# First attention chain: Grams of q in a PSUM bank of their own, and S copied by VectorE ahead of the first Exp

## The chip, the cores and the metric

The kernel runs on one core of one Trainium2 chip. The metric is device time in microseconds (us), the median of several runs. Engines are named as in the profile: PE is TensorE's matmul, PEld its weight load, DVE is VectorE, ACT is ScalarE, POOL is GpSimd, SP is SyncE.

## The reference

Four batches b of q, k, v, each 6336 x 256 in float32. Per batch a cross-covariance attention over the 256 channels, and then a highway layer over all 25344 rows:

```
qn = q / (norm(q, axis=1) + 1e-6);  kn = k / (norm(k, axis=1) + 1e-6)
a  = softmax(kn.T @ qn / tau)                     # 256 x 256 for each batch
x  = v @ a
out = T*H + (1-T)*x,  H = relu(x @ w_h),  T = sigmoid(x @ w_t + b_t)
```

## The kernel before, in words

**Tiles.** A batch is 49 slices of 128 rows and a remainder of 64 rows. Loads of q, k and v come in groups of slices (lists QG and VG); GpSimd issues them, and they turn float32 into float16 on the way. Groups of q and of k each go through a ring of 4 tiles, groups of v through a ring of 3. A load into a used tile waits until TensorE has read the tile's earlier contents.

**Scores.** For each slice, `emit_score` (L219) adds two matmuls of 256 columns to S = k.T q (L230), and four of 128 columns to the Gram matrices, two for k (L234) and two for q (L239). Only the diagonals of the Grams are used: they are the squared norms. S fills one PSUM bank, and all four Gram blocks share another bank, G. The last TAIL[0] = 6 slices of batch 0 are taken part by part: first all their q Grams (12 matmuls), then their k Grams (12), then their S (12), so that work on the norms can start before S is complete. For the later batches a part of the squares is summed by ScalarE, GpSimd and VectorE instead (L449, L455, L462).

**The chain of a batch** (`make_chain`, L493) turns S and G into the weights `mr`:

- `nq` and `norms`: VectorE reads the two diagonals of q, and of k (L503).
- `root`: for batch 0 ScalarE takes the square roots (L527), for the other batches GpSimd does.
- `ssb`: ScalarE copies S from PSUM to SBUF (L520).
- `invs`: VectorE adds 1e-6 and takes the reciprocals (L540, L543).
- `table`: ScalarE loads the table of Exp (L491), with a small activation to force it.
- `cq`: TensorE spreads 1/norm of q over the partitions (L549). `logits`: VectorE multiplies S by it (L558).
- `exps`: Exp on ScalarE (L575). `softmax`: VectorE divides by the row sums (L586, L589).
- `at`, `atc`, `ah`, `ahc`: transposes of the weights, and their product with w_h and w_t (L600, L611, L619, L630). Then `back` loads the table of Sigmoid.

**Slots.** After a batch's chain its rows come out in 25 slots of two slices: transposes of v (L293) and their copy to SBUF (L307), then twelve matmuls into the tiles zbank, h and x (L317), Sigmoid on ScalarE (tt, L358), refilling zbank with the bias (L361), two products on VectorE (o, L366; ux, L376), a subtraction on GpSimd (L399), and stores of 1 MB from SP (L416).

**PSUM.** Eight banks: z0, z1, vT (transposes), S and G (batch 0), hx1 and hx2 (S and G of the later batches), and hx0. The tiles cq, at, ah, h and x take whichever of the free banks was freed earliest; the list `banks` (L333) starts with hx0, and S and G of batch 0 join it once `ssb` and `norms` have read them (L1130).

**Order.** Nothing is ordered by hand alone: a planner at the end of the function runs through time in steps of 0.01 us, with a length for each task (for instance 0.62 for `ssb` on ScalarE, L650) and a model of the DMA queue, and emits each engine's instructions in the order in which it would start them. Tasks of a chain stand in a queue per engine and leave it strictly in order; `add` appends them. So ScalarE's chain queue of batch 0 is: root of q, ssb, root of k, table, exps, ... On the chip each engine then executes its own list in that order, and waits where the data is later than the planner thought.

Of the kernel before, what the change touches and what calls it, by code (L numbers as in the profile page):

```python
# [11 lines left out]
f32 = mybir.dt.float32  # L12
# [3 lines left out]
P = 128  # L16
# [44 lines left out]
def kernel(  # L61
# [11 lines left out]
    nc = tc.nc  # L73

    B, N, C = q.shape
# [11 lines left out]
    def spans(*sizes):  # L87
# [37 lines left out]
    psum_pool = ctx.enter_context(  # L125
        tc.tile_pool(name="psum", bufs=1, space=bass.MemoryType.PSUM)
    )
# [4 lines left out]
    def pair_of(t):  # L132
        b, i = divmod(t, NPAIR)
        return b, PAIRS[b][i]

    pairsets, unit_of = [], {}
    for t in range(NSLOT):
        b, i = pair_of(t)
# [17 lines left out]
    PE_LAG, LAG, TO_PE = 0.20, 0.08, 0.10  # L156
# [34 lines left out]
    def tile_of(kind, b, s):  # L191
        if s == NS:
            return tiles["rem", kind][:, b, :]
        groups = (VG if kind == "v" else QG)[b]
        g = group_of(groups, s)
        return tiles[kind, b, g][:, s - groups[g][0], :]
# [13 lines left out]

    S_t, G_t = {}, {}

    squares = {
        (kind, b, j + m) for b in RUNS for kind in "qk" for j in RUNS[b][kind] for m in range(CH)
# [2 lines left out]
    def emit_score(b, j, parts, first, last):  # L219
        if first:  # L220
            tags = ("S", "G") if b == 0 else ("hx1", "hx2")
            S_t[b] = psum_pool.tile([P, 2, C], f32, tag=tags[0], name=f"S{b}")
            G_t[b] = psum_pool.tile([P, 4, P], f32, tag=tags[1], name=f"G{b}")
        nr = REM if j == NS else P
        kk, qq = tile_of("k", b, j), tile_of("q", b, j)
        S, G = S_t[b], G_t[b]
        for c in range(2):
            kc = kk[0:nr, bass.ts(c, P)]
            if "s" in parts:
                nc.tensor.matmul(  # L230
                    S[:, c, :], kc, qq[0:nr, :], start=first and c == 0, stop=last and c == 1
                )
            if "k" in parts:
                nc.tensor.matmul(  # L234
                    G[:, c, :], kc, kc, start=begins(b), stop=False, skip_group_check=True,
                )
        for c in range(2 if "q" in parts else 0):
            qc = qq[0:nr, bass.ts(c, P)]
            nc.tensor.matmul(  # L239
                G[:, 2 + c, :], qc, qc, start=begins(b), stop=False, skip_group_check=True  # L240
            )

    begun = set()

    def begins(b):
        if b in begun:
            return False
        begun.add(b)
        return True

    score, grams, score_tasks, last_score = {}, {}, [], {}
# [78 lines left out]
        def free(self, now):  # L330
            return all(t.end is not None and t.end + LAG <= now for t in self.until)

    banks = [Bank("hx0")]  # L333
    handed = []

    def free_bank(now):
# [153 lines left out]
    def preload_table(func):  # L490
        nc.scalar.activation(out=dummy, in_=ones32[:, 0:1], func=func)  # L491

    def make_chain(b):  # L493
        st = {}
        T = {}
        def norms(kind):
            def emit(e):
                if "n2" not in st:
                    st["n2"] = work_pool.tile([P, 4], f32, tag="n2", name=f"n2_{b}")
                o = 2 if kind == "q" else 0  # L500
                for i in (o, o + 1):
                    junk = work_pool.tile([P, P], f32, tag="junk", bufs=1, name=f"junk{b}_{i}")
                    nc.vector.scalar_tensor_tensor(  # L503
                        out=junk, in0=G_t[b][:, i, :], scalar=0.0, in1=ident0,
                        op0=AluOp.bypass, op1=AluOp.mult, accum_out=st["n2"][:, i : i + 1],
                    )
            return emit
# [9 lines left out]

        def ssb(e):
            st["ssb"] = work_pool.tile([P, 2, C], f32, tag="ssb", bufs=1, name=f"ssb{b}")
            nc.scalar.copy(out=st["ssb"], in_=S_t.pop(b))  # L520

        def root(kind):
            def emit(e):
                o = 2 if kind == "q" else 0
                dst, src = nrm[:, o : o + 2, 0], st["n2"][:, o : o + 2]
                if b == 0:
                    nc.scalar.activation(out=dst, in_=src, func=Act.Sqrt)  # L527
                else:
                    nc.gpsimd.tensor_tensor(
                        out=dst, in0=src, in1=half[:, 0:2], op=AluOp.pow  # L530
                    )
            return emit

        def invs(kind):
            def emit(e):
                o = 2 if kind == "q" else 0
                if "inv" not in st:
                    st["inv"] = work_pool.tile([P, 4], f32, tag="inv", name=f"inv{b}")
                inv = st["inv"][:, o : o + 2]
                nc.vector.tensor_reduce(  # L540
                    out=inv, in_=nrm[:, o : o + 2, :], axis=mybir.AxisListType.X, op=AluOp.add
                )
                nc.vector.reciprocal(out=inv, in_=inv)  # L543
            return emit
# [88 lines left out]
        def add(key, engine, length, emit, after, bank=None):  # L633
            T[key] = Task(("chain", b, key), engine, length, emit, after)
            T[key].wants_bank = bank is not None
            T[key].readers = bank
            queues[engine + ".chain"].append(T[key])
            return T[key]
# [7 lines left out]
        engine, length = ("ACT", 0.25) if b == 0 else ("POOL", 0.75)  # L646
        for kind, n in (("q", "nq"), ("k", "norms")):
            add(("root", kind), engine, length, root(kind), [(T[n], LAG)])
            if kind == "q":
                add("ssb", "ACT", 0.62, ssb, [(last_score[b], PE_LAG)])  # L650
        add(("invs", "q"), "DVE", 0.4, invs("q"), [(T["root", "q"], LAG)])
        add(("invs", "k"), "DVE", 0.4, invs("k"), [(T["root", "k"], LAG)])
        add("table", "ACT", 1.5, lambda e: preload_table(Act.Exp),
            [(T["root", "k"], 0.0)] if b == 0 else [(T["invs", "q"], EXP_LAG)])
        add("cq", "PE", 4 * MM(C), pe_cq, [(T["invs", "q"], TO_PE)],
            bank=lambda: [T["softmax", 0], T["logits", 1]])
# [12 lines left out]
        for c in range(2):  # L669
            add(("at", c), "PE", 2 * MM(P), pe_at(c), [(T["softmax", c], TO_PE)],  # L670
                bank=lambda c=c: [T["atc", c]])
        for c in range(2):
            add(("atc", c), "DVE" if c == 0 else "ACT", 0.4, at_copy(c), [(T["at", c], PE_LAG)])
            add(("ah", c), "PE", 2 * MM(2 * C), pe_ahat(c), [(T["atc", c], TO_PE)],
                bank=lambda c=c: [T["ahc", c]])
# [44 lines left out]
    for t in range(NSLOT):  # L720
        i = pair_of(t)[1]
# [39 lines left out]
    for b in range(B):  # L761
        i = 0
# [35 lines left out]
    ident0 = const_pool.tile([P, P], f32, tag="ident0")  # L798
# [8 lines left out]
    btb = const_pool.tile([P, 2, C], f32, tag="btb")  # L807

    def seed_banks():
        btp = psum_pool.tile([P, 2, C], f32, tag="hx0", name="btp")  # L810
        nc.tensor.matmul(btp[:, 0, :], ones32[0:1, :], bt_sb, start=True, stop=True)
        for u in range(2):
            nc.scalar.copy(out=btb[:, u, :], in_=btp[:, 0, :])
        for i in range(2):
            zb = psum_pool.tile([P, 2, C], f32, tag=f"z{i}", name=f"zbank{i}")
            nc.tensor.matmul(
                zb[:, :, :], zeros[:, 0:P], zeros[:, :], start=True, stop=True,
                skip_group_check=True,
            )
            nc.scalar.copy(out=zb[:, :, :], in_=btb[:, :, :])  # L820
            zbank.append(zb)
# [24 lines left out]
    for b in range(B):  # L846
        queues["PE.S"] += make_scores(b)
        chains[b] = make_chain(b)
# [4 lines left out]
    for t in range(NSLOT):  # L853
        b, i = pair_of(t)
# [94 lines left out]
    def head(n):  # L949
        return queues[n][ptr[n]] if ptr[n] < len(queues[n]) else None  # L950
# [172 lines left out]
    while True:  # L1123
        if not dma.advance(now, STEP):
            idle_dma += STEP
        if not setup_done[0] and score[0, 3].end is not None and score[0, 3].end < now:
            seed_banks()
            preload_table(Act.Sqrt)
            setup_done[0] = True
        for b, key, tag in ((0, "ssb", "S"), (0, "norms", "G"), (B - 1, "ssb", "hx1"),  # L1130
                            (B - 1, "norms", "hx2")):
            if tag not in handed and chains[b][key].end is not None:
                handed.append(tag)
                banks.append(Bank(tag))
                banks[-1].until = [chains[b][key]]
        for e, f in (("PE", step_pe), ("ACT", step_act), ("DVE", step_dve),
                     ("POOL", step_pool), ("SP", step_sp)):
            while free[e] <= now and f(now):
                pass
        finished = all(ptr[n] == len(queues[n]) for n in queues) and nload[0] == len(loads) and \  # L1140
            all(s.dma.end is not None for s in store_tasks)
        if finished:
            break
        now += STEP
        assert now < 600, [(n, head(n).name) for n in queues if head(n) is not None]
# [38 lines left out]
```

## Time and profile before

| what | us |
|---|---|
| median of 3 runs (lowest to highest) | 270.42 (270.23 to 270.47) |
| time of the profiled execution | 270.2 |
| its span, first to last instruction | 268.4 |
| outside the span | 1.8 |
| TensorE clock granted, mean | 0.997 |
| PE / DVE / POOL / ACT busy | 246.2 / 207.8 / 205.3 / 192.5 |

The page of a profile gives the busy time of each engine, a row of 40 slices of the span for each (a digit is the busy share in tenths), and groups of instructions by line. Other views used here are the timeline of one engine (start, duration, line and operation, and in brackets the idle time just before it with the instruction that ended it), the waits (who waited for whom), the chain of work that ended last, in order of time, and a table of engine busy time and DMA rate by stretches of time. Matmuls overlap in the pipe, so the duration of a single one (0.27 us for 256 columns) is longer than the step from one to the next (0.11 us).

In time, batch 0's scores take the first 38 us, paced by loads; its chain runs from about 35 to 45.5 us; the first slot's matmuls begin at 45.72 us; from then on slots of one batch and scores of the next are interleaved, and the last chain (batch 3) ends at about 212 us. The last matmuls end near 263 us.

### The profile page before, as it was taken

To read this page: it belongs to the slowest core of one execution; us is meant where nothing else is said; L and a number is where in the kernel's file an instruction comes from. 1 tells how busy PE (TensorE), PEld (TensorE's weight loads), DVE (VectorE), ACT (ScalarE), POOL (GpSimd) and SP (SyncE) were. 2 spreads that over 40 slices of the span, in tenths; PEclk is the share of its full clock that TensorE was granted. 3 is DMA by queue.
4 is the path that set the end of the run, shared out by engine and by line. 5 is a ranking of instruction groups with operands and counts; after the bars stand their busy time and mean duration, and the time that the engine had idled before them with its cause. 6 is when DMAs were issued, how large, how long until landed. Compare 5 with 4: busy or idle time off the path is not lost.

```text
span 268.4 us, 6454 instructions
## 1 busy us (share of the span) xinstructions
PE 246.2 (92%) x2564; PEld 213.9 (80%) x2564; DVE 207.8 (77%) x415; ACT 192.5 (72%) x320; POOL 205.3 (76%) x182
## 2 busy tenths in 40 slices
PE   0996887899999999979999999999999999999991
PEld 0696785789989997869988987898989687989780
DVE  2000035869999999879989899899999998989895
ACT  3310026969689979869996798898867987888690
POOL 6133455489999999997899998899966485977870
PEclk9999999999999999999999999999999999999998
DMA  7999999999999999999999999999999999698436
GB/s 215 214 214 213 204 187 221 209 214 213 215 210 213 234 268 215 209 271 211 291 289 301 284 215 224 213 297 300 274 290 353 298 375 413 141 224 347 205 128 236
DMA packets 16287, 66.08 MB, mean 246 GB/s; under 512 B 1793, under 2 KB 4610, under 8 KB 13314
## 3 DMA queue, kind: packets, MB, share of 16 engines
q0 software_dynamic: 11040, 38.67, 73.2%
q1 hardware_dynamic: 4930, 26.35, 24.6%
q10 hardware_dynamic: 288, 0.66, 0.7%
q8 instruction: 20, 0.33, 0.4%
q14 instruction: 9, 0.07, 0.1%
HBM read 78.38 MB, written 25.95 MB: 389 GB/s over the span
## 4 chain that ended last, share of the span: by engine, by line
PE 39%; DMA 34%; POOL 10%; DVE 8%; issue 5%; ACT 3%; DVEq 0%; POOLq 0%; ACTq 0%
DMA k<-in_k_dram 19%; DMA v<-in_v_dram 10%; PE x L317 7%; PE zbank L317 7%; PE S L230 7%; PE h L317 7%; POOL o L399 5%; PE vtps L293 4%; DMA out_dram<-o 3%; PE G L234 3%; PE G L239 2%; DVE o L366 2%; DVE ux L376 2%; DMA qk<-in_k_dram 2%; ACT tt L358 1%
## 5 line engine op out<-in xcount | busy, mean ns | idle before, releaser
L399 POOL TENSOR_TENSOR o<-o,ux 128x1024 f32<-128x1024 f32 (+1 forms) x49 | 110.5, 2257 | 24.0 <-DVE ux L376 20.9
L317 PEld LDWEIGHTS <-vts 128*128 128x128 f16 x1200 | 111.7, 98 | 16.4 <-issue 4.3
L230 PE MATMUL S<-q,k 128*128 128x256 f16 x392 | 73.5, 278 | 13.0 <-DMA k<-in_k_dram 6.7
L358 ACT ACTIVATE tt<-zbank 128x512 f32<-128x512 f32 x100 | 59.3, 595 | 23.8 <-PE zbank L317 16.0
L366 DVE SCALAR_TENSOR_TENSOR o<-h,tt 128x512 f32<-128x512 f32 x96 | 65.8, 685 | 6.5 <-ACT tt L358 3.2
L376 DVE SCALAR_TENSOR_TENSOR ux<-tt,x 128x512 f32<-128x512 f32 (+1 forms) x104 | 68.1, 658 | 2.7 <-PE x L317 2.7
L317 PE MATMUL x<-mr,vts 128*128 128x256 f16 (+1 forms) x400 | 60.5, 273 | 0.4 <-DVE o L366 0.4
L317 PE MATMUL zbank<-mr,vts 128*128 128x256 f16 (+1 forms) x400 | 60.5, 273 | 0.0
L317 PE MATMUL h<-mr,vts 128*128 128x256 f16 (+1 forms) x400 | 60.5, 273 | 0.0
L361 ACT COPY zbank<-btb 128x512 f32<-128x512 f32 x98 | 57.6, 591 | 2.7
L230 PEld LDWEIGHTS <-k 128*128 128x128 f16 x392 | 37.6, 100 | 19.0 <-DMA k<-in_k_dram 7.9
L234 PE MATMUL G<-k 128*128 128x128 f16 x256 | 44.0, 224 | 0.7 <-DVE junk L503 0.7
L293 PE MATMUL vtps<-ident,v 128*128 128x128 f16 x392 | 38.3, 219 | 1.0 <-DVE vts L307 0.7
L307 DVE COPY vts<-vtps 128x512 f16<-128x512 f16 x68 | 28.6, 421 | 6.7 <-PE vtps L293 6.3
L293 PEld LDWEIGHTS <-v 128*128 128x128 f16 x392 | 28.7, 98 | 4.5 <-issue 1.7
L177 POOL DMA_DIRECT2D q<-in_q_dram x25 | 14.2, 568 | 23.1 <-PE G L239 18.6
L503 DVE SCALAR_TENSOR_TENSOR junk<-G,ident 128x128 f32<-128x128 f32 x16 | 4.7, 291 | 31.0 <-PE G L234 30.3
L239 PE MATMUL G<-q 128*128 128x128 f16 x216 | 28.6, 224 | 0.0
L455 POOL TENSOR_TENSOR sqq<-sqq 128x512 f32<-128x512 f32 (+1 forms) x22 | 26.4, 1204 | 0.1
L234 PEld LDWEIGHTS <-k 128*128 128x128 f16 x256 | 24.0, 101 | 1.8 <-issue 1.1
L449 ACT ACTIVATE sqq<-q 128x1024 f32<-128x1024 f16 x22 | 23.0, 1054 | 0.0
L462 DVE TENSOR_REDUCE sqq<-sqq 128x256 f32<-128x768 f32 x22 | 22.6, 1027 | 0.0
(78 smaller groups left out, 214.9 us busy)
## 6 DMA issues: line engine op xcount, KB each, us to landing
out_dram<-o SPq DMA_DIRECT2D x23, 1024.0 KB, 9.8
v<-in_v_dram POOLq DMA_DIRECT2D x11, 768.0 KB, 17.2
q<-in_q_dram POOLq DMA_DIRECT2D x7, 768.0 KB, 14.9
k<-in_k_dram POOLq DMA_DIRECT2D x7, 768.0 KB, 19.3
q<-in_q_dram POOLq DMA_DIRECT2D x9, 512.0 KB, 13.3
k<-in_k_dram POOLq DMA_DIRECT2D x9, 512.0 KB, 15.2
v<-in_v_dram POOLq DMA_DIRECT2D x4, 832.0 KB, 19.0
q<-in_q_dram POOLq DMA_DIRECT2D x4, 256.0 KB, 13.0
```

Source lines behind the costliest of these rows:

```text
L230: nc.tensor.matmul(S[:, c, :], kc, qq[0:nr, :], start=first and c == 0, stop=last and c == 1)
L234: nc.tensor.matmul(G[:, c, :], kc, kc, start=begins(b), stop=False, skip_group_check=True,)
L239: nc.tensor.matmul(G[:, 2 + c, :], qc, qc, start=begins(b), stop=False, skip_group_check=True)
L293: nc.tensor.transpose(ps[:, u, c, 0:r], vt[0:r, bass.ts(c, P)], ident[0:r, 0:r])
L307: cp(out=sb, in_=ps)
L317: nc.tensor.matmul(dst[0:r, u, :], vT_t[t][:, u, kt, 0:r], mr[:, kt, off : off + C], start=(not seeded and kt == 0 and (u == 0 or i == NPA ...
L358: nc.scalar.activation(out=tts[t], in_=zbank[t % 2], func=Act.Sigmoid)
L361: nc.scalar.copy(out=zbank[t % 2], in_=btb)
L366: nc.vector.scalar_tensor_tensor(out=ot[pr, o0 + us.start : o0 + us.stop, :], in0=hx["h", t][pr, us, :], scalar=0.0, in1=tts[t][pr, us, :] ...
L376: nc.vector.scalar_tensor_tensor(out=uxs[n][pr, 2 * half + us.start : 2 * half + us.stop, :], in0=tts[t][pr, us, :], scalar=1.0, in1=hx["x ...
L399: ins = sub.tensor_tensor(out=dst, in0=dst, in1=uxs[n][pr, us, :], op=AluOp.subtract)
L455: nc.gpsimd.tensor_tensor(out=sq[:, 1 : 1 + half, :], in0=sq[:, 1 : 1 + half, :], in1=sq[:, 1 + CH - half : 1 + CH, :], op=AluOp.add,)
```

## The change

For batch 0 alone:

- The Grams of q get a tile Gq of their own in the bank hx0; those of k stay in G. Each of the two banks has its own first matmul with `start`. For later batches Gq is the second half of G, as before.
- hx0 is no longer free from the start: it joins the list of banks once `nq` has read Gq.
- `ssb` is done by VectorE, and stands in VectorE's chain queue behind the two `invs`; ScalarE's chain queue is then root of q, root of k, table, exps, ...
- The tile btp, which holds the bias while the seeds are made near 11 us, moves from hx0 to the bank of the transposes, vT.

```diff
@@ emit_score
             G_t[b] = psum_pool.tile([P, 4, P], f32, tag=tags[1], name=f"G{b}")
+            Gq_t[b] = G_t[b][:, 2:4, :] if b else psum_pool.tile(
+                [P, 2, P], f32, tag="hx0", name=f"Gq{b}"
+            )
...
-                    G[:, c, :], kc, kc, start=begins(b), stop=False, skip_group_check=True,
+                    G[:, c, :], kc, kc, start=begins(b, "k"), stop=False, skip_group_check=True,
...
-                G[:, 2 + c, :], qc, qc, start=begins(b), stop=False, skip_group_check=True
+                Gq[:, c, :], qc, qc, start=begins(b, "q"), stop=False, skip_group_check=True
...
-    def begins(b):
-        if b in begun:
+    def begins(b, kind):
+        bank = (b, kind if b == 0 else "")
+        if bank in begun:
             return False
-        begun.add(b)
+        begun.add(bank)
         return True
@@ banks
-    banks = [Bank("hx0")]
+    banks = []
@@ norms
-                        out=junk, in0=G_t[b][:, i, :], scalar=0.0, in1=ident0,
+                        out=junk, in0=Gq_t[b][:, i - 2, :] if i > 1 else G_t[b][:, i, :], scalar=0.0, in1=ident0,
@@ ssb
-            nc.scalar.copy(out=st["ssb"], in_=S_t.pop(b))
+            cp = nc.vector.tensor_copy if e == "DVE" else nc.scalar.copy
+            cp(out=st["ssb"], in_=S_t.pop(b))
@@ make_chain
-            if kind == "q":
+            if kind == "q" and b > 0:
                 add("ssb", "ACT", 0.62, ssb, [(last_score[b], PE_LAG)])
         add(("invs", "q"), "DVE", 0.4, invs("q"), [(T["root", "q"], LAG)])
         add(("invs", "k"), "DVE", 0.4, invs("k"), [(T["root", "k"], LAG)])
+        if b == 0:
+            add("ssb", "DVE", 0.7, ssb, [(last_score[b], PE_LAG)])
@@ seed_banks
-        btp = psum_pool.tile([P, 2, C], f32, tag="hx0", name="btp")
+        btp = psum_pool.tile([P, 2, C], f32, tag="vT", name="btp")
@@ planner's loop
-        for b, key, tag in ((0, "ssb", "S"), (0, "norms", "G"), (B - 1, "ssb", "hx1"),
+        for b, key, tag in ((0, "nq", "hx0"), (0, "ssb", "S"), (0, "norms", "G"), (B - 1, "ssb", "hx1"),
                             (B - 1, "norms", "hx2")):
```

## The prediction

> **What bounds the kernel now.** I read the page's first two parts, then the chain of work that ended last, then the timelines of the engines around batch 0's chain, the waits, and the DMA rate by stretches.
>
> ```profile
> span 268.4 us, 6454 instructions
> PE 246.2 (92%) x2564; PEld 213.9 (80%) x2564; DVE 207.8 (77%) x415; ACT 192.5 (72%) x320; POOL 205.3 (76%) x182
> ...
> PE   0996887899999999979999999999999999999991
> ...
> DMA  7999999999999999999999999999999999698436
> ```
>
> The DMA engines are full from the start to slice 34 (about 228 us), and PE is full from about 57 to 260 us. PE's few idle stretches lie ahead of 58 us, and one at 117 us. So what happens in batch 0's chain matters in two ways: PE's idle time there is part of the total, and any gap in the DMA queue is never made up.
>
> The chain of work that ended last goes straight through the place of the change:
>
> ```profile
> 35.83 0.31 DVE junk L503 x2
> 36.14 0.02 issue
> 36.16 0.31 DVE junk L503 x2
> 36.47 0.04 issue
> 36.51 0.61 PE G L234 x8
> 37.12 0.23 PE S L230 x2
> 37.35 0.29 issue
> 37.64 0.55 POOL q L177
> ...
> 40.27 17.15 DMA v<-in_v_dram
> ```
>
> PE stops its k Grams after four of twelve (35.80 us) until VectorE has read q's diagonals (36.46 us), because all Grams lie in one bank. The first S matmuls of the tail, at 37.12 us, free a ring tile for the loads that GpSimd issues from 37.64 us on. The rate of the DMA by stretches (columns: stretch, us; PE, PEld, DVE, ACT, POOL busy; clock; DMA share; GB/s) shows that these loads come late:
>
> ```profile
> 37.00:38.00 1.00, 1.00 (x13) 0.90 (x10) 0.78 (x6) 0.00 (x0) 0.36 (x1) 1.00 1.19 210
> ...
> 39.00:39.50 0.50, 0.50 (x8) 0.47 (x7) 0.28 (x3) 0.48 (x3) 0.50 (x2) 1.00 0.96 85
> 39.50:40.00 0.50, 0.50 (x9) 0.45 (x7) 0.50 (x3) 0.50 (x1) 0.50 (x2) 1.00 1.02 143
> 40.00:40.50 0.50, 0.47 (x8) 0.35 (x6) 0.19 (x1) 0.49 (x2) 0.50 (x2) 1.00 1.02 190
> ```
>
> ScalarE's timeline of the chain (start, duration, line, operation, idle before):
>
> ```profile
> 36.49 0.20 ACT L527 ACTIVATE nrm<-n 128x2 f32<-128x2 f32 x1 [22.09 <-DVE junk L503]
> 38.47 0.58 ACT L520 COPY ssb<-S 128x512 f32<-128x512 f32 x1 [1.77 <-PE S L230]
> 38.95 0.21 ACT L527 ACTIVATE nrm<-n 128x2 f32<-128x2 f32 x1
> 39.17 1.28 ACT L491 ACT_TABLE_LOAD   x1
> 40.47 0.20 ACT L491 ACTIVATE dummy<-ones 128x1 f32<-128x1 f32 x1
> 40.57 0.46 ACT L575 ACTIVATE cq<-ssb,inv 128x256 f32<-128x256 f32 x1
> ```
>
> The root of k could run at 37.8 us (VectorE's last read of k's diagonals ends at 37.79), but stands behind the copy of S and ends at 39.16. The table follows, and the first Exp starts when the table is there: the logits had been ready since 39.87 us (the first of two, 39.46 + 0.41).
>
> **What the Trainium skill says.** PSUM — Partial Sum Buffer, section PSUM bank collisions raise a hardware error: PSUM is to be guarded by bank, not by address. The trace agrees: k's Grams wait 0.72 us for a read of other columns of G. The same page, Engine vs sequencer instructions: the queues of ScalarE and VectorE are strictly first in, first out. The trace agrees: the root of k waits 1.2 us behind `ssb`. ScalarE: Activation LUTs, What ACT_TABLE_LOAD costs: 1.28 us for the load and 1.38 us for a drain. The load is 1.28 us here; of the drain nothing shows, the first Exp starts 1.40 us after the load does. I use 1.40.
>
> **The change part by part**, against the profiled execution (270.2 us, span 268.4; the median 270.42 is 0.2 higher, and I move the result by that).
>
> *Bank of its own for q.* q's Grams end at 35.56. VectorE reads them at once instead of at 35.83, for 0.63 us (35.83 to 36.46), so until 36.22. PE goes on without the stop: twelve k Grams took 0.24 + 0.61 us in two pieces, so they end near 36.35 at the latest instead of 37.12. That is 0.7 to 0.8 us for PE, k's norms, S and the loads freed by S. k's diagonals are then read from 36.3 to 36.95; the root of k, 0.2 us, ends near 37.17 instead of 39.16, as nothing stands ahead of it in ScalarE's queue. The table is there at 37.2 + 1.40 = 38.6 instead of 40.57.
>
> *Copy of S on VectorE.* S took 1.31 us (37.12 to 38.43), so it ends near 37.65. VectorE first does the two `invs` (0.35 us each, done near 37.65), then the copy. The trace has no such copy; the nearest row is VectorE's conversion of 128x512 from PSUM (L630), 0.69 us; VectorE: DVE Perf Modes (section on the TRN2 errata) gives (120 + 512) cycles at 0.96 GHz, an estimate of 0.66. I take 0.69: 37.65 to 38.34. Queued behind it are only the logits, and they need cq too. cq started 0.16 us after S's end, behind four matmuls of batch 1, and took 0.66: now 37.8 to 38.45. So the copy costs nothing, hidden by cq with 0.1 us to spare; were S or cq earlier, it would show with at most 0.69. ScalarE is rid of 0.58 us. The first logits are ready at 38.47 + 0.41 = 38.9, and what is late next is no longer the table (38.6) but this. First Exp: 38.9 instead of 40.57, **1.67 us earlier**, and softmax and `at` with it.
>
> *After the chain.* Before, PE stood 0.78 us at 43.00 us with scores of batch 1 whose k had not landed, and the second `at` waited behind them (43.34; its data was ready at 42.46). If the planner now puts `at` ahead, up to 0.88 more is won; I count 0. Slots 0 and 1 can start near 44.0 instead of 45.72: their v landed at 39.86. Slot 2 needs the v that lands at 45.4.
>
> *DMA queue.* The rates above are short of 210 GB/s by 125, 67 and 20 GB/s in three half microseconds: 0.5 us of a full queue lost. With the loads from 37.64 on issued 0.7 us earlier, most of that goes: I take **0.45 us** earlier landings for all that follows.
>
> *hx0 and btp.* No one took hx0 ahead of cq (38.59) in the chain, and Gq is read by 36.22: 0. btp's two readers on ScalarE end at 11.75 us and the first transposes start at 40.09: 0. The number of matmuls is the same, DVE gains one instruction, ACT loses one; no DMA is added.
>
> **How much of it reaches the end.** PE later waits on landings: for k at 53.29 (0.88 us), v at 57.47 (0.2) and k at 117.36 (1.64). These move by 0.45 only. A PE that is 1.67 ahead just waits longer there, unless the planner, which sees the head start too, puts slots in between; there is such work (at 69 us, when the next v lands, slot 11 was still to be done; at 80.5 three slots). So the bounds are 0.45 (the landings alone) and 1.67 (all). I take the middle, **1.1 us**: 270.2 - 1.1 = 269.1, and 269.3 for the median.
>
> **Rivals.**
> *Absorbed.* PE's lead is all waited away at 53 and 117 us, and the DMA gap closes only half, since other things than S may hold the loads back. For it: PE starts on k's scores at 53.29, 65.59 and 76.78, each within 0.3 us of a landing (53.3, 65.3, 76.5). Against: slots were always left over. It gives 0 to -0.45, so 270.2.
> *Slower: GpSimd's queue.* The change shifts the planner's clock, so tasks change places all the way. GpSimd is full from 58 to 96 us, and loads stand in its queue between subtractions of 2.36 us; the k that PE waits for at 117.36 was issued at 98.02. If one more subtraction gets ahead of it, k lands up to 2.36 us later and PE waits in full: -0.45 + 2.36 = +1.9, so 272.3. It decides from the point where the loads outstanding no longer cover the delay. For it: around 95 us the rate jumps from 215 to over 400 GB/s, so loads had run short there and a store had the queue alone. Against: an earlier chain lets subtractions start earlier too (the first was at 50.69, waiting 4.2 us for data).
> *All of it kept.* The whole 1.67 us survives and a part of the 0.88 does not: 270.42 - 1.7 = 268.7.
>
> **Chances.** Forecast 0.40 (range 268.8 to 269.95), of which 0.37 is faster; absorbed 0.20; slower 0.33; all kept 0.07. This kernel's measurement tells 0.2% (0.54 us) from no change. So faster 0.44, same 0.23, slower 0.33. The range takes in all kept and reaches to the slower rival's full price: 268.5 to 272.3. That the change does nothing is no rival: the stop at 35.80 and the place of `ssb` follow from bank and queue.
>
> **What would show it.** No wait of PE for L503 at 36.5; loads at 36.9 instead of 37.64 and no dip near 39 us; root of k before 37.5; first Exp near 38.9; first slot near 44; k for 117 us landing near 116.9. I am wrong if the waits at 53 and 117 us grow by what the chain gains, or if loads after 60 us are issued later than before.

## The result and the profile after

The changed kernel took **272.94 us** (median, 272.55 to 273.63) where the kernel before took 270.45 in the same measurement: a ratio of 1.0096, 95% interval 1.0073 to 1.0119. It is slower, and above the range that was forecast. Measured once more on another occasion it gave 1.0082 (1.0062 to 1.0101). The ratios are estimated from the single executions, those more than 1.5% above their kernel's fastest left out, so they can differ by about 0.1% from the ratio of the medians. The profiled execution took 272.7 us, 2.5 more than that of before, with the same mean clock (0.995).

From the page of the changed kernel: span, busy time of the engines, and the rows of PE and DMA in 40 slices.

```profile
span 270.9 us, 6452 instructions
...
PE 246.6 (91%) x2564; PEld 214.0 (79%) x2564; DVE 211.0 (78%) x416; ACT 193.2 (71%) x319; POOL 205.8 (76%) x182
...
PE   0997898799999999999997979998999999999991
...
DMA  7999999999999999999999999999997999699436
```

PE's work is the same; it is its idle time that grew. Two new 7s stand in slices 22 and 24 (142 to 149 and 156 to 162 us) and an 8 in slice 28 (183 to 190 us), far from batch 0's chain and in what was a full stretch before; the 7 at 117 us (slice 18) is gone. DVE's busy time is 3.2 us larger with one instruction more, which will matter below.

The chain itself, from the changed kernel's timeline of all engines (start, duration, engine, line, operation, idle before):

```profile
35.75 0.83 PE L237 MATMUL G<-k 128*128 128x128 f16 x12
...
37.10 0.55 POOL L177 DMA_DIRECT2D q<-in_q_dram  x1 [2.40 <-PE S L233]
...
37.36 0.20 ACT L532 ACTIVATE nrm<-n 128x2 f32<-128x2 f32 x1 [0.54 <-DVE junk L507]
...
37.58 1.28 ACT L495 ACT_TABLE_LOAD   x1
...
37.93 0.69 DVE L525 COPY ssb<-S 128x512 f32<-128x512 f32 x1
...
38.06 0.66 PE L554 MATMUL cq<-ident_tau,inv 128*128 128x128 f32 x4
...
38.76 0.75 DVE L563 TENSOR_TENSOR ssb<-ssb,cq 128x256 f32<-128x256 f32 x2
...
39.61 0.48 ACT L580 ACTIVATE cq<-ssb,inv 128x256 f32<-128x256 f32 x1 [0.53 <-DVE ssb L563]
...
44.38 0.60 PE L321 MATMUL zbank<-mr,vts 128*128 128x256 f16 x4
```

The twelve k Grams run without a stop, the root of k is 1.6 us earlier, the copy of S lies under `cq`, the first Exp starts at 39.61 instead of 40.57 us, and the first slot's matmuls at 44.38 instead of 45.72. In this execution the first loads had landed 0.34 us later (5.97 instead of 5.63 us), and the last q Grams end at 35.91 instead of 35.56. Counted from there, the first Exp is 1.31 us and the first slot 1.69 us earlier. The change does what it says. The dip in the DMA rate near 39 us (last column, GB/s) is smaller too, 180, 198 and 205 where 85, 143 and 190 were:

```profile
39.00:39.50 0.50, 0.50 (x9) 0.47 (x6) 0.50 (x2) 0.08 (x1) 0.50 (x2) 1.00 1.15 180
39.50:40.00 0.50, 0.21 (x3) 0.04 (x1) 0.01 (x1) 0.39 (x1) 0.50 (x2) 1.00 1.12 198
40.00:40.50 0.50, 0.40 (x4) 0.23 (x4) 0.23 (x2) 0.50 (x3) 0.50 (x2) 1.00 1.13 205
```

PE's waits from 40 us to the end (waited for: us in total, times, longest), first before, then after:

```profile
PE S L230 <- DMA k<-in_k_dram: 3.3, 3, 1.6
PE vtps L293 <- DVE vts L307: 0.7, 2, 0.5
PE at L600 <- DVE mr L589: 0.6, 1, 0.6
PE x L317 <- DVE o L366: 0.4, 1, 0.4
```

```profile
PE x L321 <- DVE o L370: 2.7, 2, 1.4
PE at L605 <- DVE at_sb L616: 1.4, 1, 1.4
PE S L233 <- DMA k<-in_k_dram: 1.1, 2, 0.9
PE vtps L297 <- ACT vts L311: 0.9, 1, 0.9
```

The longest waits were for landings before; after, most of the waiting is for other engines. Summed over PE's gaps of more than 0.12 us:

| stretch | before | after |
|---|---|---|
| 34 to 130 us | 0.72 + 0.52 + 0.56 + 0.78 + 0.88 + 1.64 = 5.10 | 0.32 + 0.55 + 0.30 + 0.23 + 0.26 + 0.95 + 0.89 = 3.50 |
| 130 to 200 us | 0.36 + 0.40 = 0.76 | 1.43 + 0.40 + 0.22 + 1.38 + 1.22 = 4.65 |

So by 130 us the change had gained 1.6 us, and between 143 and 184 us it lost 3.9. Net 2.3, with the 0.35 us of the start 2.6; the span grew by 2.5. A second profile of the changed kernel (r1 below) shows the same three large stops, of 1.38, 1.38 and 1.09 us. Three places make the loss, and the chain of work that ended last runs through all three:

```profile
120.81 22.33 DMA k<-in_k_dram
143.22 1.06 ACT sqk L453
...
157.36 1.01 DVE mr L594
158.37 1.72 issue
...
173.48 9.56 DMA out_dram<-o
183.16 0.70 DVE o L370
183.91 0.60 PE x L321 x4
```

**Place A, 143 us.** ScalarE and VectorE and PE of the changed kernel, from the timeline:

```profile
143.22 1.06 ACT L453 ACTIVATE sqk<-k 128x1024 f32<-128x1024 f16 x1 [3.23 <-DMA k<-in_k_dram]
144.19 0.58 ACT L362 ACTIVATE tt<-zbank 128x512 f32<-128x512 f32 x1
...
144.80 0.69 DVE L370 SCALAR_TENSOR_TENSOR o<-h,tt 128x512 f32<-128x512 f32 x1 [2.73 <-ACT tt L362]
...
145.54 0.60 PE L321 MATMUL x<-mr,vts 128*128 128x256 f16 x4 [1.43 <-DVE o L370]
```

The Square of the first k group of batch 3 (k3_0 from here on) stands ahead of a Sigmoid (tt) in ScalarE's list. The group lands at 143.14 us, so ScalarE stands for 3.23 us with a Sigmoid queued behind whose data is there; VectorE waits for the Sigmoid, PE for VectorE. Before, a Sigmoid and a refill of zbank stood ahead of that Square, and it waited for nothing, as k3_0 landed at 143.05:

```profile
143.51 1.05 ACT L449 ACTIVATE sqk<-k 128x1024 f32<-128x1024 f16 x1
```

**Place B, 157 us.** VectorE and GpSimd at the softmax of batch 2's chain:

```profile
156.77 0.48 DVE L594 TENSOR_SCALAR mr<-cq,rinv 128x256 f16<-128x256 f32 x1
156.96 2.37 POOL L403 TENSOR_TENSOR o<-o,ux 128x1024 f32<-128x1024 f32 x1
...
157.36 2.81 DVE L594 TENSOR_SCALAR mr<-ssb,rinv 128x256 f16<-128x256 f32 x1
...
159.28 0.72 POOL L459 TENSOR_TENSOR sqk<-sqk 128x256 f32<-128x256 f32 x1
```

The two halves of the softmax are the same instruction; the first reads PSUM (cq), the second SBUF (ssb). The first takes 0.48 us, the second 2.81: it ends at 160.17, just after GpSimd's two instructions, which end at 159.33 and 160.00. Before, this second half took 0.77 us:

```profile
159.68 0.77 DVE L589 TENSOR_SCALAR mr<-ssb,rinv 128x256 f16<-128x256 f32 x1
```

PE stands 1.38 us before the second transpose of the weights; what ends that wait is VectorE's copy at_sb (160.09 us), which stands behind the long instruction in VectorE's list. The long one appears as busy time and in no list of waits.

**Place C, 184 us.** Held up by B, GpSimd's later subtractions are late, so (e5 below bears it out) a store starts at 173.48 instead of 172.46 and lands at 183.04 instead of 181.47; VectorE's next o needs that tile and waits 1.93 us, PE 1.22 (before: 0.95 and 0.40).

### The profile page after: what moved, and what is told of

Read it like the earlier page. It is cut to its first block, busy times and chain, and to the rows that moved or that the text cites. A ratio compares the mean times of both kernels' runs of the same rounds, so it can differ in the third digit from the quotient of the medians.

```text
span 270.9 us, 6452 instructions
## 1 busy us (share of the span) xinstructions
PE 246.6 (91%) x2564; PEld 214.0 (79%) x2564; DVE 211.0 (78%) x416; ACT 193.2 (71%) x319; POOL 205.8 (76%) x182
## 4 chain that ended last, share of the span: by engine, by line
PE 60%; DMA 24%; DVE 5%; POOL 5%; issue 4%; ACT 1%; DVEq 0%; POOLq 0%; ACTq 0%
DMA k<-in_k_dram 18%; PE x L321 11%; PE zbank L321 11%; PE h L321 11%; PE S L233 10%; PE vtps L297 6%; DMA out_dram<-o 4%; PE G L237 3%; DMA qk<-in_k_dram 2%; POOL o L403 2%; PE G L242 2%; DVE ux L380 1%; DVE o L370 1%; PE Gq L242 1%; PE G L516 1%
## 5 line engine op out<-in xcount | busy, mean ns | idle before, releaser
L507 DVE SCALAR_TENSOR_TENSOR junk<-Gq,ident 128x128 f32<-128x128 f32 x2 | 0.6, 292 | 29.4 <-PE Gq L242 29.4
L453 ACT ACTIVATE sqk<-k 128x1024 f32<-128x1024 f16 x17 | 17.8, 1054 | 4.2 <-DMA k<-in_k_dram 4.2
```

The source lines that it names most:

```text
L453: nc.scalar.activation(out=area(n)[:, 1:, :], in_=tiles[kind, b, g][:, o : o + CH, :], func=Act.Square)
```

## The experiments

**Theories.** Theory 1: the changed instructions are good, and the changed order, which the planner makes for all engines from 38 us on, costs the time; narrowed after the first four runs (1a in the expectations) to the two places A and B. The rivals: that the bank or the copy itself costs something, or that any head start of PE's is waited away at landings, so that mending A and B brings nothing beyond them. Runs of one group below were made on the same chip and share the runs of before.

### Instructions and order apart

e1 takes only the bank of its own and leaves the order as before (hx0 joins the banks as before). e2 has both parts, but the planner is told nothing of the copy's new engine; the order is that of before. e3 has the instructions of before in the order of the changed kernel. e4 has the copy of S on VectorE in the order of the changed kernel, and q's Grams in the common bank.

```diff
# e2, against the changed kernel
-    banks = []
+    banks = [Bank("hx0")]
...
-            cp = nc.vector.tensor_copy if e == "DVE" else nc.scalar.copy
+            cp = nc.vector.tensor_copy if b == 0 else nc.scalar.copy
...
-            if kind == "q" and b > 0:
+            if kind == "q":
...
-        if b == 0:
-            add("ssb", "DVE", 0.7, ssb, [(last_score[b], PE_LAG)])
...
```

```diff
# e3, in the planner's list of the changed kernel: ssb emits copy, root, invs and table as before
-            nc.vector.tensor_copy(out=st["ssb"], in_=S_t.pop(b))
+            nc.scalar.copy(out=st["ssb"], in_=S_t.pop(b))
+            if b == 0:
+                root("k")(None)
+                invs("k")(None)
+                preload_table(Act.Exp)
...
```

> Only the bank: q's Grams of batch 0 in hx0, btp in vT, the copy of S left on ScalarE and the planner's inputs untouched, so that every engine's order is that of the kernel before. Theory 1 (the changed order of the later work costs the 2.5 us; the new instructions by themselves gain): no stop of PE at 36.5, the loads from 37.6 on issued 0.5 to 0.7 us earlier, time 269.6 to 270.3. Theory 2 (the new instructions cost it: the second bank, or the copy on VectorE): if the bank is to blame, near 272.9, else 270.4.

> The bank and the copy of S on VectorE, but the planner still counts the copy as ScalarE's with its old length, so that all other instructions keep the order of the kernel before. Theory 1: first Exp about 1 us earlier than before, time 269.2 to 270.3. Theory 2: as slow as the changed kernel, 272.5 to 273.5.

> The converse: one bank for all Grams, S copied by ScalarE ahead of k's root and the Exp table behind it, as before, but the planner is told of the changed chain, so that all later work has the order of the changed kernel. Theory 1: as slow as the changed kernel or slower, 272.5 to 274.5. Theory 2: 270.4.

> The copy of S on VectorE alone, with the planner told so (order of the changed kernel), and all Grams in one bank as before. Theory 1: the stop of PE at 36.5 is back, time 272.5 to 274. Theory 2 with the bank to blame: 270.4; with the copy to blame: 272.9.

| kernel | instructions | order | median us | ratio to before (95%) |
|---|---|---|---|---|
| e1 | bank | before | 270.32 | 0.9989 (0.9960 to 1.0018) |
| e2 | bank and copy | before | 270.58 | 0.9997 (0.9981 to 1.0014) |
| e3 | before | after | 272.11 | 1.0050 (1.0030 to 1.0070) |
| e4 | copy | after | 272.09 | 1.0055 (1.0032 to 1.0078) |

**The new order costs by itself, the new instructions by themselves don't.** All of the change in the order of before makes no difference that can be told; none of it in the order of after costs 0.5%. (e3 and e4 came out 0.4 us below what theory 1 had expected at the least, e2 0.3 above what it had expected at the most.) The changed kernel costs 0.8 to 1.0%, so a part comes only where the two meet, though the intervals of e3 and of its repetition r1 still touch.

In e2 the earlier chain ends at once in a wait: PE stands 1.32 us at 43.05 us for the first k group of batch 1, ahead of the second `at`. That is the wait of 0.78 us that the prediction had seen, grown by what the chain had gained. But this is not where the gain ends. PE's list in e2 is that of before, matmul by matmul, so its lead can be read off: the score matmul that waits for k at 117.36 us before starts at 115.86 in e2, 1.5 us earlier; the x that starts at 182.30 before starts at 182.91, 0.6 us later. In between e2 meets the same three places:

```profile
144.59 1.06 ACT L453 ACTIVATE sqk<-k 128x1024 f32<-128x1024 f16 x1 [2.51 <-DMA k<-in_k_dram]
...
159.16 1.51 DVE L594 TENSOR_SCALAR mr<-ssb,rinv 128x256 f16<-128x256 f32 x1
...
182.91 0.60 PE L321 MATMUL x<-mr,vts 128*128 128x256 f16 x4 [0.96 <-DVE o L370]
```

PE stops 0.60 us behind the Sigmoid that the Square held up (146.90), 0.58 for a reduction soon after (149.39), 0.40 at the softmax and 0.96 here: 2.54 us between 130 and 200 us, against 0.76 before. (k3_0 landed at 144.50 us in that execution, 1.4 later than in the one of before.) So the places lie in the order of before too, and a PE that comes early meets them there; the new order makes them dearer.

e3 also splits A from B. VectorE, GpSimd and PE of e3:

```profile
156.28 2.37 POOL L401 TENSOR_TENSOR o<-o,ux 128x1024 f32<-128x1024 f32 x1
...
156.88 2.59 DVE L595 TENSOR_SCALAR mr<-ssb,rinv 128x256 f16<-128x256 f32 x1
...
158.60 0.72 POOL L457 TENSOR_TENSOR sqk<-sqk 128x256 f32<-128x256 f32 x1
...
159.86 0.27 PE L606 MATMUL at<-ident,mr 128*128 128x128 f16 x2 [1.38 <-DVE at_sb L617]
```

Place B is there in full, and C with 0.76 us (0.52 in e4); at A PE loses nothing in e3 and e4, though the Square waits 1.71 and 1.86 us. There PE comes later (the ux of slot 36 starts at 135.39 us in e3, at 134.56 in the changed kernel), and k3_0 lands earlier: at 142.45 us in e3 and 142.22 in e4, at 143.14 in the changed kernel. So B and C come with the order alone (2.1 us in e3), and A's 1.4 us comes on top when PE is early against that landing; which of the two counts for more these traces don't separate.

### The two places mended one by one

r1 is the changed kernel again. e5 takes batch 2's second softmax half from VectorE to ScalarE, with all lists else as they were. e6 gives only the Square of k3_0 a landing allowance 2.5 us longer, and this one instruction moves in ScalarE's list, behind one more Sigmoid and its refill of zbank. e7 has both.

```diff
# e5, in softmax
+                if b == 2 and c == 1:
+                    nc.scalar.activation(
+                        out=mr_t[b][:, c, 0:C], in_=st["e", c], func=Act.Copy,
+                        scale=st["rinv"][:, c : c + 1],
+                    )
+                    return
```

```diff
# e6, where the Square gets its landing allowance
-        sq.after.append((task_of_load[kind, b, g], LAND))
+        sq.after.append((task_of_load[kind, b, g], LAND + (2.5 if (b, j, kind) == (3, 0, "k") else 0)))
```

> The changed kernel again, beside the three that mend it. Both theories: 272.0 to 273.5, slower than before by 0.5 to 1.0%.

> The changed kernel with one instruction on another engine: in batch 2's softmax the second normalisation (128x256 in SBUF to 128x256 in SBUF, 2.81 us on VectorE while GpSimd subtracts, 0.35 us when GpSimd is idle) is done by ScalarE; the order of all others is unchanged. Theory 1a (that instruction is held until GpSimd's two instructions end, and PE's second transpose of the weights waits 1.38 us for it): the wait near 160.6 goes to below 0.4, time 0.8 to 1.4 us below the changed kernel. Theory 1b (the lead of PE is limited by landings anyway, and the next wait takes its place): the wait goes, but PE waits as much longer near 184 for the store that frees an output tile; time within 0.4 us of the changed kernel.

> The changed kernel with one instruction moved in ScalarE's order alone: the Square of batch 3's first k group comes 2.6 us later in the plan (143.6 instead of 141.0), behind the Sigmoids that it held up for 3.2 us while its k had not landed. Theory 1a: PE's waits at 145.5 and 147.4 (1.43 and 0.40 us) go, time 1.2 to 1.8 us below the changed kernel. Theory 1b: they go, but the time is within 0.4 us of the changed kernel.

> Both edits on the changed kernel. Theory 1a: waits of PE between 140 and 165 us below 1.0 us in sum, time 269.3 to 270.5, at or below the kernel before. Theory 1b: 271.8 to 273, with longer waits near 184 us and later.

| kernel | median us | ratio to before (95%) |
|---|---|---|
| r1 | 272.81 | 1.0082 (1.0062 to 1.0101) |
| e5 | 270.51 | 0.9996 (0.9972 to 1.0020) |
| e6 | 270.20 | 0.9977 (0.9963 to 0.9991) |
| e7 | 270.13 | 0.9980 (0.9966 to 0.9993) |

One instruction out of 6452, given to another engine or moved in its list, takes back all that the change cost, 2.3 us with e5 and 2.6 with e6; both together take back no more (2.7). e5 gave more than I had expected of it: B took C along, as its store landed at 180.9 us. In e5 ScalarE does the second half in 0.49 us, with GpSimd as busy as before:

```profile
158.29 0.49 ACT L595 ACTIVATE mr<-ssb,rinv 128x256 f16<-128x256 f32 x1
```

In that execution A cost PE nothing, since PE was later (first ux at 49.2 instead of 47.1 us), so e5 doesn't test A. e6 doesn't touch B, and yet B is smaller there. VectorE, GpSimd and PE of e6:

```profile
155.40 2.35 POOL L403 TENSOR_TENSOR o<-o,ux 128x1024 f32<-128x1024 f32 x1 [0.70 <-DVE ux L380]
...
156.82 1.08 DVE L594 TENSOR_SCALAR mr<-ssb,rinv 128x256 f16<-128x256 f32 x1
...
157.72 0.77 POOL L459 TENSOR_TENSOR sqk<-sqk 128x256 f32<-128x256 f32 x1
...
163.75 0.40 PE L297 MATMUL vtps<-ident,v 128*128 128x128 f16 x4 [0.89 <-DMA v<-in_v_dram]
```

With A gone all engines are elsewhere: the second half meets only the end of the subtraction and costs PE 0.34 us. What stops PE next is the landing of batch 2's first v at 163.7 us: 0.89 us in e6, 0.87 in e7, 0.53 in e5. So there is little for the second mend to add: with A mended little of B is left, in e7 PE still waits 0.52 us for ScalarE's half there, and all three run into that landing. The Square itself still waits for its landing, 1.12 us in e6 and 0.81 in e7, but the Sigmoid that PE was about to need is ahead of it.

### Does the early Square alone do it, and is there more to gain

e8 is e2 with both mends. e9 is the kernel before with nothing of the change but an earlier Square of k3_0 (the allowance of e6 with -2.0; one reduction on VectorE moves along). e10 is e6 with the Square of k1_0, batch 1's first k group, planned later too, since in the changed kernel it delays ScalarE's copy of transposes for slot 3, for which PE stands 0.95 us at 50.63. r2 is e6 again.

```diff
# e9, in the kernel before; e10 the same in the changed kernel, with {("k", 3, 0): 2.5, ("k", 1, 0): 12.0}
-        sq.after.append((task_of_load[kind, b, g], LAND))
+        late = {("k", 3, 0): -2.0}
+        sq.after.append((task_of_load[kind, b, g], LAND + late.get((kind, b, j), 0)))
```

> The instructions of the change in the order of before, with the second normalisation of batch 2 on ScalarE and the Square of k3_0 later. Theory: the earlier chain gains nothing in the order of before, since PE then waits for k1_1 near 43 us, and the end is set by the landing of v2_0 near 163.5 us; so 270.2 to 270.6, no better than the order of before without the mends. Rival: the two late waits (Square 2.51 us, normalisation 1.51 us) had eaten a gain of the chain in that order too; then about 1 us under the kernel before, 269.5.

> The kernel before, with nothing of the change, but the Square of k3_0 placed one tt and one seed earlier in ScalarE's order (planned 1.2 us earlier; one reduction on VectorE moves with it). Theory that a Square placed ahead of its landing is enough to cost the kernel its time: k3_0 lands at about 143.1, ScalarE's sequence stands about 2 us for it, o of the next slot waits, PE stops about 1 us near 145 and the time rises by 1 to 2.5 us, 271.5 to 273. Rival, that the cost needs the whole changed order (the PE lead that makes slots earlier, and the hold of VectorE at 157 us): within 0.5 us of before, 270.2 to 271.

> The changed kernel with the Square of k3_0 later and the Square of k1_0 planned behind ScalarE's copy of slot 3's transposes (many later tasks change places with it). Locally, both theories: PE's wait of 0.95 us at 50.6 us goes and the slots 3 and 4 are earlier by about that. Theory that what PE gains ahead of 130 us is waited away at landings near 163.5: 270.0 to 270.4, as with the one Square alone (270.2). Rival, that the lead lost at 50.6 us is kept to the end: 269.3. Since many tasks move, a time above 270.4 would tell only that order matters by itself.

> The changed kernel with only the Square of k3_0 later, once more: 270.2, ratio to the kernel before 0.998, if the first result holds; the same as before (0.999 to 1.001) if it was chance.

| kernel | median us | ratio to before (95%) |
|---|---|---|
| e8 | 270.19 | 0.9974 (0.9956 to 0.9992) |
| e9 | 271.01 | 1.0002 (0.9978 to 1.0026) |
| e10 | 269.85 | 0.9963 (0.9943 to 0.9982) |
| r2 | 270.27 | 0.9964 (0.9945 to 0.9983) |

The kernel before had a median of 270.96 us in this group, with a wider scatter than elsewhere, so the ratios count here.

**e9: my theory in its simple form falls.** ScalarE waits for k3_0 as expected:

```profile
143.12 1.06 ACT L449 ACTIVATE sqk<-k 128x1024 f32<-128x1024 f16 x1 [1.56 <-DMA k<-in_k_dram]
```

The Sigmoid behind it starts at 144.09 us and o at 144.70, hardly before the 144.19 and 144.80 of the changed kernel. But PE has no gap near 145 us, and the time is that of before. In e9 PE's list has eight score matmuls there (143.55) and the first matmuls of the next slot, ahead of anything that needs this o. In the changed kernel the x of the slot comes next, and its eight score matmuls stand behind it (145.97). So A takes two things: a Square ahead of its landing, and PE early at a matmul that depends on it, with the filling work already done or queued behind. e2 has both in the order of before, with its Sigmoid at 145.55 us, and there PE stops (0.60 us).

**e10** moves a part of PE's wait to the next landing. Its profiled execution was 5 us longer than the median of its runs, so I read only its beginning. ScalarE copies the transposes at 46.82 us, PE's wait at 50.6 is gone, and PE stops here instead:

```profile
52.85 1.16 PE L233 MATMUL S<-q,k 128*128 128x256 f16 x9 [0.95 <-DMA k<-in_k_dram]
```

In r2 this wait is 0.66 us, so of the 0.95 us some 0.3 come back here. By its time, e10 equals r2 (0.9963 and 0.9964): the lead of slot 3 doesn't show at the end. Many later tasks change places with it, so where it goes isn't shown.

**The best version** is the changed kernel with the Square of k3_0 one Sigmoid later: faster than the kernel before in both measurements, 0.9977 (0.9963 to 0.9991) and 0.9964 (0.9945 to 0.9983), some 0.6 to 1.0 us, or 0.4 and 0.7 by the medians. Its fastest executions are no faster (269.73 against 269.60 us, 269.75 against 269.29); what it lacks are the slow ones: each time its 22 executions lie within 0.9 and 1.1 us, the 75 of before within 4.7 and 6.9. Why it scatters less is open.

e8 reaches the same in the old order. Whether that is more than e2 without the mends (0.9997, up to 1.0014) the intervals leave open, but it lies nearer to the rival in its expectation than to the theory: its median is 0.77 us under that of before in the same group, and PE's stops between 130 and 200 us sum to 0.98 us instead of e2's 2.54. It is not e2 with two instructions moved alone, since the later Square shifts other tasks, and batch 2's second half then reads PSUM.

## Why the prediction was wrong

**Right.** *The bank of its own*: PE's stop of 0.72 us is gone. *The root of k* was forecast for 37.17, which is 1.61 us after the end of q's Grams; it ended 1.65 after it (37.56 - 35.91). *The copy of S* was to take 0.69 us and to be hidden by `cq`: 0.69, from 37.93 to 38.62, and `cq` ended at 38.72. The cover was as thin as stated. *The table* is no longer late: Exp waits for the logits, as said. *The first slot*, forecast for 44.0, came at 44.38 with a start 0.35 late. That it fits so well is luck: Exp was 0.36 us less early than forecast (below), and the planner put the second `at` ahead of batch 1's scores (41.57 instead of 43.34 us), a gain that the prediction named and counted as 0. *DMA queue*: forecast 0.45 us earlier landings. The rate between 39 and 40 us recovered (189 GB/s instead of 114). The last v issued ahead of the chain landed 0.16 us later than before (39.98 instead of 39.82); after it v came at 57.26 instead of 57.42, k at 76.17 instead of 76.45 and at 104.13 instead of 104.42, so counted from there 0.32 to 0.45 us earlier.

**A small miss.** *First Exp*: 1.31 us earlier instead of 1.67, relative to the end of q's Grams. I had let Exp start after the first of the two logits; it started at 39.61, 0.10 us after the second (38.76 + 0.75). Three figures in the working are off and change nothing: the k Grams' pieces sum to 36.41 and not 36.35, the v of slots 0 and 1 landed at 39.82 and not 39.86, and at 57.47 us it is the weight load that was idle for 0.22 us, the matmuls only 0.05.

**The step that failed is "How much of it reaches the end".** It put the gain between 0.45 us (landings alone) and 1.67 (all), and took the middle, 1.1. Its ends were thought of as bounds, on the ground that PE's head start could only be kept or waited away. At 130 us this was even right: 1.6 us less idle time. But PE's head start brought PE to where other engines were not ready (e2 shows that in the order of before), and the planner's changed order put two instructions into worse places: 1.4 us at A, 1.4 at B and 1.2 at C (0.4 of it there before), and 0.6 in two short stops after A (147.41 and 149.55 us), which e3 has too (0.40 and 0.23). What reached the end was -2.5 us, outside both ends. This step treated landings as the only thing that PE can run into.

**The rivals.** *Slower by GpSimd's queue* had the right sign, by luck nearly the right time (272.3), and the right trigger (the planner's clock shifts and tasks change places all the way), but the wrong place. The k for 117 us was issued at 97.80 instead of 98.02 and landed at 115.61 instead of 117.31; PE's wait of 1.64 us there vanished. Later loads were issued later, as that rival had it (105.65 became 109.40, with a landing 1.4 us later; 118.88 became 120.81, with the same landing), but PE waited for neither. The tasks that did the harm were ScalarE's and VectorE's. *Absorbed* is wrong for the changed kernel: the waits at 53 and 117 us did not grow (0.89 us instead of 0.88, and none instead of 1.64). In e2 the chain's gain is gone at 43 us, but the 1.5 us that PE has at 117 us are lost to other engines. A landing stops PE where A or B is mended, that of v at 163.7 us. *All kept* held until 130 us and no further.

**What was not weighed.** For A the queue order of ScalarE was in my own text: the PSUM page of the Trainium skill, section Engine vs sequencer instructions, has ScalarE's queue strictly first in, first out, and I used it for the root of k alone. Here it makes 3.23 us out of one early Square. I looked for late loads, not for instructions that stand in front of a landing. For B the page SBUF — State Buffer, section Who interferes with whom, states that VectorE's `tensor_scalar` can use a port pair that it shares with GpSimd, and that the second of the two to issue then blocks fully. The runs agree in all they show:

| kernel | second half (SBUF) us | its end after a GpSimd instruction's end |
|---|---|---|
| e1 (GpSimd's instruction ended 0.16 us after its start) | 0.35 | 0.19 |
| before | 0.77 | 0.16 |
| e6 | 1.08 | 0.15 |
| e4 | 2.17 | 0.16 |
| e3 | 2.59 | 0.16 |
| changed | 2.81 | 0.16 |
| e2 | 1.51 | 0.16 (after GpSimd had issued a load, 160.51 us) |

The first half, from PSUM, took 0.48 us in each of these. The second half has a control in every trace: it reads SBUF (ssb) only where the planner had no free bank for the output of Exp. In batch 3 it had one (e), and in the changed kernel the half took 0.48 us there in the middle of a subtraction:

```profile
210.71 2.34 POOL L403 TENSOR_TENSOR o<-o,ux 128x1024 f32<-128x1024 f32 x1 [0.72 <-DVE ux L380]
...
211.77 0.48 DVE L594 TENSOR_SCALAR mr<-e,rinv 128x256 f16<-128x256 f32 x1
```

That it is the shared port is the page's explanation, not a thing that these runs show; they show that the instruction from SBUF ends just after one of GpSimd's and that the half from PSUM, or on ScalarE, does not. B was to be found in the profile of before: the two halves took 0.48 and 0.77 us, with GpSimd full.

What stays open: by how much A alone lengthens the changed kernel wasn't separated, since taking A away also shifts B.

## What to carry to other kernels

An earlier start in a kernel whose order is planned from modelled times is two changes: the instructions, and a new order for all that follows; run each without the other before judging either. And look where a lead is lost, not only whether the time is the same: e2's equal time hid 1.5 us gained and 2.1 lost again. Ask for each instruction that waits on a landing what stands behind it on an in-order engine, and how far ahead PE may be before it needs that. Where such a change costs time, look in the trace for the first new gap of the busiest engine and move only that instruction: here one Square turned +0.8 to +1.0% into -0.2 to -0.4%.

## What the hardware did that I had not expected

- A VectorE instruction from SBUF lasted 0.35 to 2.81 us with the same shape, by what GpSimd did, and the same half from PSUM 0.48 us beside GpSimd too; it counts as busy, so VectorE's busy time rose by 3.2 us: 2.0 of them are this instruction's, 0.7 the copy's. In the changed kernel, e3 and e4 it was held through two GpSimd instructions on end; in e6 it ended between two (157.90 us), and the second of them took 0.77 instead of 0.72 us.
- The same late Sigmoid, 0.1 us apart, cost PE nothing in e9 and 1.43 us in the changed kernel. The price of an in-order wait is not its length: it depends on what PE has queued ahead of its next dependence. In the changed order waits of 1.71, 1.86 and 1.91 us (e3, e4, e5) cost PE nothing, and one of 3.23 us cost 1.43.
